# Attention and gated FFN on one core: the value products of units 2 to 11 summed by row tile, the two sums added on VectorE

## The chip, the cores and the metric

The kernel runs on one core of one Trainium2 chip. The metric is the time of one execution on the device in microseconds; a measurement is the median of several runs. The profile shows one execution of its own. Its span runs from the first to the last instruction of the program, and the time of the same execution is a little longer, because of what lies around the program.

The names of the engines are those of the profile: PE (TensorE, matrix products) and PEld (its weight loads), DVE (VectorE), ACT (ScalarE), POOL (GpSimd) and SP (SyncE); the last two issue DMAs here, POOL the loads and SP the transposes and the stores.

## The reference

Block-sparse attention over 4 batches, 8 heads, 768 positions and 64 columns a head, and then a gated feed-forward network (FFN) on the 3072 tokens of 512 columns:

```python
scores = scale * np.matmul(q, k.transpose(0, 1, 3, 2))
# mask: a block's neighbours, the first and last block, three sampled blocks a row
scores = np.where(mask, scores, -1000000000.0)
attn = np.exp(scores - np.max(scores, axis=-1, keepdims=True))
attn = attn / (np.sum(attn, axis=-1, keepdims=True) + 1e-09)
attn_out = np.matmul(attn, v)
...
gate = 1.0 / (1.0 + np.exp(-(x @ w_gate)))     # x: 3072 x 512, w_gate and w_val: 512 x 1536
out = gate * (x @ w_val) @ w_out               # w_out: 1536 x 512
```

## The kernel before

**Units and pairs.** The work is cut into 12 units of 256 query rows (4 batches of 3 units), and each unit into 4 pairs of heads. A pair has three score steps. A step (`Step`) multiplies keys by queries into a PSUM unit of two banks (`qk`, L553), takes the exponential on ACT into a tile `P` (`exp`, L576) and multiplies `P` by the 0/1 mask on DVE (`mul`, L581; unit 0 has its mask added in the scores instead). When the three steps of a pair are done, the value product (`Pair.pv`, L602) multiplies `P` by the values, which carry a column of ones, so that column 64 of each product is the sum of the row. The product has 65 columns for each of 2 heads and 2 row halves. `norm` (L620) takes the reciprocal of the sums on DVE and multiplies them in, reading PSUM and writing the fp16 tile `x16`. For units 2 to 11 a DMA transpose on SP's queue (`Pair.xbar`, L673) then turns `x16` into the FFN's input `xT`; for units 0 and 1 PE transposes it.

**FFN.** `Ffn.f` (L742) makes the gate and the value product of a group of columns, ACT takes a tanh, DVE combines the two (`gate`). `Ffn.y` (L826) multiplies by the last weights, and ACT or DVE copies the result out of PSUM. Units 4 to 11 go through the FFN two at a time.

**Row tiles.** Nearly all matmuls use 64 of the 128 rows of the array, so that two run side by side, one on each half: a row tile. The two tiles running together must write different PSUM banks, and every sum needs both row tiles. So a product is done in two halves (`turns`, L345): in the first half row tile 0 writes bank 0 and row tile 1 writes bank 1, in the second they change banks and add to what is there. Ahead of the second half an empty instruction waits until the first half has left the array (L349). For the value product, each half is 24 matmuls (`value`, L641: two PE tasks of 24, and other tasks may stand between them). In units 0 and 1 the product uses whole columns of 128 rows instead (`whole`, L362).

**PSUM.** There are four units of two banks (`units_ps`, L308). A PE task that begins a product takes one, written in the order as `:slot`; the task marked `free` gives it back. For the value product that is `norm`.

**The order.** Nothing is scheduled at run time. `ORDER` (L40) is a list of the 1173 tasks in the order in which each engine issues its own: a number, a letter where a task may run on one of two engines (`A` for ACT, `D` for DVE), the PSUM slot after a colon, and after `@` the task that a DMA load is held for. `j3`, `j3s` and the like are matmuls on a dummy tile ahead of the real work. Each engine works through its list in turn, and a task waits until what it needs is done. The list was made ahead of time by a planner; the costs written into `plan.add` (for instance 0.66 for a mask product) are what the planner counts with and do nothing at run time.

Of the kernel before, what the change touches and what calls it, by code (L numbers as in the profile page):

```python
# [13 lines left out]
f32 = mybir.dt.float32  # L14
# [8 lines left out]
NT = S // 128  # L23
# [14 lines left out]
FFN_LAG = 3  # L38
VW = 96
ORDER = """  # L40
j3 j3 j3 j3 j3 j3 j3 5A 8D j3 j3s j3s 0 j3s j3s 9:0 j3s j3s 11A 10D j3s 1:1 j3s j3s j3s 12:2 2 3:0
13A 6:1 j3s 32:2 4D 7A 15:1 34:3 33 16D 17:0 18D 97:1 35 30:2 98D 78:0 31 79D 40:3 20:1 22:0 41
36:2 23D 21D 117:0 92@36 37 44:3 118D 25:1 45 54:0 26D 76:2 77D 46:1 55 80:3 27:2 81D 47 50:0 28D
74:3 19 64:1 51 75D 48:2 65 24 66:3 49 60:0 56:1 67D 61 52:2 29 58:3 14 57 53D 89:0 59 86:2 68:1
87 38:3 69D 90 93:1 39 62:2 108:3 94 42:0 63A 109 43D 95:2 70:1 96D 102:0 71D 111:2 103 110 140:3
126:1 105@140 88 112 104 141 84:0 122:2 113 127 85A 142 130:3 128 132:0 123 129 131 72:1 119:2
99:3 73D 237@102 133 120 124 147:1 91 134 100 135 154:2 101 148 157:0 171:3 158 149 155 164:1 172
143:0 156 176:2 144 159 173 165 145 150:0 231:3 177 190:1 170@231 232 178 189@154 121 146@86 161:2
191 125@143 174:3 151A 192 217@108 162 115:0 114@99 175 244:1 186:2 116 204:3 187 205 138 245 139
211:0 82:2 206 212 83D 214:1 233 183:2 136:0 215 218 137D 246 193:0 184 219 194D 152 200:1 216 153  # L50
179:0 220 201 160@200 180D 229 167:2 255:0 166 168 202 272:1 221A 185 256 223A 188 234:2 230 239
307:3 257 181 195 235 273 262 258 197:2 240 213 308 274 198 275 248:0 182 309 199 241:1 249 242
310 196 268:2 169 225:3 250 252:1 224 269 251 226 222 253 227 263 106:0 207:2 107A 254 318:3 208
319 315:0 289:1 209 247@315 316 236 265:3 293:2 260 266 320 261 300:0 290 243 301 238 267 276:3
291 282:0 210 294 283 292 279 277 295 303:1 335:0 278 304 296 297 285:3 336 286 305 228 362:1 163
337 287 363 331:2 264 328:3 348 302 332 270 344:1 329 349 333 345 359:2 284 322:3 203@359 350 364
360 288@197 323 351D 353A 311:1 271@265 426:2 324 312 321@331 427 341:0 373:3 313 342 330 325
397:2 408:1 346 374 398 343 387:0 409 317 370:2 259 375 405:1 388 400@54 406 376 386@40 371 389
355:3 365@157 419:1 390 432@108 356 407 443:0 411@197 420 372 444 347@405 361 433:2 421 334@30 298
357 366:0 306@164 399 377 380:3 434 422 381 299 410 367 435 428 412:1 368 436 454:3 369 413 455  # L60
382 450:2 414 326 471:0 451 472 415 447:3 338 452 401:1 473 440:0 478:2 391 402 441 448 403 479
470 378 457:0 449 280 458 445 394:1 383:2 438 460 395 392 439 456 461 384 396 327 429:0 524:1 385
462 430 459 423 416:2 525 442 484:0 354 465D 463A 481:1 281 417 431 482 485 418 474:3 488:1 486
# [4 lines left out]
583 547 537:3 563:2 314 570 538 586 638:0 552 564 571 539 572 639 565 566:3 577:2 575A 573D  # L68
556@566 595:0 567 576 604 446@32 466 609:1 568 712@86 616:3 596 358 691@64 617 608@46 610 597
641@164 630:3 598 611 622@64 592:0 612 658@282 578 404 593 706:1 579 631 707 594 635:2 561 627:0  # L70
632 543@635 588:1 636 633 628 623:3 629 654 670:2 589 671 618 688:0 624 590 689 591 642:2 453 625
619:1 640 659:0 620 637 643 626 605:1 708 663:3 644 569@605 621 606 660 587@183 645 726@40 681:1
661 709:2 664 676@265 710 662 682 548 665 673:0 549 692:2 683 674 711 699:1 599 666 655:0 693 607
# [3 lines left out]
750 739 751:3 748 752 837:1 650 742 669 749 838 757:3 745D 760 764:0 743D 823:1 758 824 782 667  # L77
759 765 825 826:2 798:1 839 767 827 614 580 734:0 615 799 768 828 753 735 761:2 651 806:1 769 797
762 800 790:0 807 756 862:2 791 736 770A 779 772A 771 819:1 719 763 792 809:3 863 793 810 820 705
# [5 lines left out]
909:0 912 905 910 928 922 913 937 911 855:2 978:0 896 914 856 888 946:1 917A 915D 919:2 947 979  # L85
857 920 929:3 921 938 1027:0 932 875:2 1028 930 948 918 1012:1 876 1013 931 877 970:0 893 1024:2
952:1 939 1025 966 940 971 959:2 953 941 960 942A 1055:0 973:1 961 1056 944D 1001:2 1057 967:0 974
# [6 lines left out]
1074 1081 1093 1089 1082 1065 1094 1083 1084 1095 1085D 1108:1 1096D 1104:0 1098D 1097 1087D 1099  # L94
# [3 lines left out]
1153 1163:0 1156A 1159 1154A 1157 1164 1155 1165 1160 1166 1167 1168:1 1161 1169 1170 1162 1171  # L98
1172
"""  # L100
GAP, PV_HALF, F_HALF, Y_ONE = 0.3, 0.36, 0.875, 0.216
WIDE, WIDE_PV = 1, 2


# [53 lines left out]
def kernel(  # L158
# [231 lines left out]
    def before(nm, i):  # L390

        j = i - len(rings[nm])
        return used[nm][j] if j >= 0 else []
# [196 lines left out]
    class Pair:  # L590
# [50 lines left out]
        def value(self):  # L641
            deps = self.products + [vdone[self.b, self.p]]
            if self.n < WIDE_PV:
                a = plan.add(
                    [(PE, 2 * PV_HALF)],
                    lambda eng: self.pv(None),
                    deps,
                    take=self.bank,
                    ops=48,
                    wide=True,  # L650
                )
# [474 lines left out]
```

## Time and profile before

| | |
|---|---|
| median of 3 runs (lowest, highest) | 281.54 us (281.45, 283.77) |
| the profiled execution, its time | 281.49 us |
| the profiled execution, its span | 279.7 us |
| PE busy | 271.4 us, 97% of the span, 5007 matmuls |
| DVE busy | 188.7 us, 67%, 387 instructions |
| ACT busy | 188.7 us, 67%, 237 instructions |
| granted TensorE clock | 1.00 all through |
| value products of units 2 to 11 | 1920 matmuls of 64 rows by 65 columns |
| last value product starts | at 238.8 us |

How to read it: the 1.8 us between the time and the span lie around the program. Busy PE time is not PE at its peak, because matmuls overlap and their ends are modelled; what a stretch of matmuls costs is read from the distance between starts. A busy share of 67% for DVE and ACT is an average over a start in which data is still arriving, a long middle part in which attention and FFN are mixed, and an end that is FFN alone, where both are nearly idle.

### The profile page before, as it was taken

What the parts mean: (1) busy time and instruction counts of PE and PEld (TensorE: products, weight loads), DVE (VectorE), ACT (ScalarE), POOL (GpSimd) and SP (SyncE); (2) the same over time, 40 slices, a digit from 0 to 9 for tenths busy, and PEclk for the clock granted to TensorE, in tenths of its full rate; (3) what the DMA queues carried; (4) which work ended last, traced back from release to release, by engine and by line L of the source; (5) the groups of instructions that cost most, each with busy time, mean ns of one, the idle gap of its engine ahead of it and who ended that gap; (6) DMA issues with size and microseconds to landing.
All of it is one profiled execution on the core that took longest, in us unless ns stands there. A gap on an engine that the chain in (4) does not pass through costs nothing.

```text
span 279.7 us, 11113 instructions
## 1 busy us (share of the span) xinstructions
PE 271.4 (97%) x5007; PEld 207.6 (74%) x5007; DVE 188.7 (67%) x387; ACT 188.7 (67%) x237; POOL 47.4 (17%) x70
## 2 busy tenths in 40 slices
PE   8799999989999999999999999999999999999995
PEld 4577786977898799658899889888766567555543
DVE  4578777877877988867796897567735787243311
ACT  4899868879957988976877793877779651013411
POOL 7876443010480000071400000000000000000000
PEclk9999999999999999999999999999999999999999
DMA  7999999994699864169596443210110011430003
GB/s 150 180 195 197 200 205 197 149 186 87 83 138 163 102 147 101 40 128 189 72 175 90 58 106 96 68 58 2 41 38 2 0 22 23 143 150 4 0 2 150
DMA packets 56680, 28.93 MB, mean 103 GB/s; under 512 B 33044, under 2 KB 53676, under 8 KB 56632
## 3 DMA queue, kind: packets, MB, share of 16 engines
q0 software_dynamic: 21552, 13.93, 35.9%
q1 hardware_dynamic: 34628, 14.02, 25.7%
q8 instruction: 39, 0.64, 0.9%
q10 hardware_dynamic: 452, 0.26, 0.3%
q14 instruction: 9, 0.07, 0.1%
HBM read 28.47 MB, written 6.29 MB: 124 GB/s over the span
## 4 chain that ended last, share of the span: by engine, by line
PE 92%; DMA 2%; POOL 2%; ACT 1%; DVE 1%; issue 1%; DVEq 0%
PE m L343 91%; DMA k<-in_k_dram 2%; ACT P L577 1%; PE m L463 1%; POOL k L225 1%; POOL q L225 1%; POOL v L225 0%; DVE ysb L856 0%; DVE mask L287 0%; POOL e L262 0%; ACT ysb L854 0%; PE m L458 0%; DVE x L623 0%; DVE e L208 0%; ACT ysb L897 0%
## 5 line engine op out<-in xcount | busy, mean ns | idle before, releaser
L577 ACT ACTIVATE P<-m 128x1024 f16<-128x1024 f32 x144 | 142.2, 1025 | 31.8 <-PE m L343 28.5
L343 PE MATMUL m<-xT,wv 64*128 64x512 f16 (+2 forms) x720 | 136.7, 327 | 0.0
L343 PE MATMUL m<-xT,wg 64*128 64x512 f16 (+2 forms) x720 | 135.4, 327 | 0.0
L583 DVE TENSOR_TENSOR P<-P,mask 128x1024 f16<-128x1024 f16 x132 | 86.0, 686 | 4.4 <-ACT P L577 3.9
L343 PEld LDWEIGHTS <-wg 64*128 64x128 f16 (+1 forms) x720 | 66.6, 94 | 14.1 <-issue 1.5
L343 PEld LDWEIGHTS <-wv 64*128 64x128 f16 (+1 forms) x720 | 66.5, 94 | 11.4 <-issue 0.3
L772 DVE SCALAR_TENSOR_TENSOR ht<-th,m 128x512 f16<-128x512 f32 x72 | 49.2, 686 | 37.4 <-ACT th L769 36.5
L343 PE MATMUL m<-wo,ht 64*128 64x512 f16 (+2 forms) x564 | 71.7, 372 | 0.0
L769 ACT ACTIVATE th<-m 128x512 f32<-128x512 f32 x72 | 42.9, 598 | 40.7 <-PE m L343 37.5
L343 PE MATMUL m<-qT,kT 64*128 64x256 f16 x576 | 56.5, 269 | 0.3 <-issue 0.2
L343 PEld LDWEIGHTS <-P 64*128 64x128 f16 (+1 forms) x2112 | 46.9, 94 | 5.8 <-issue 1.3
L343 PE MATMUL m<-vex,P 64*128 64x65 f16 (+1 forms) x2112 | 48.1, 190 | 0.9 <-issue 0.9
L343 PEld LDWEIGHTS <-ht 64*128 64x128 f16 (+1 forms) x564 | 35.5, 94 | 17.9 <-issue 1.3
L343 PEld LDWEIGHTS <-kT 64*128 64x128 f16 x576 | 33.6, 94 | 9.3 <-issue 1.1
L622 DVE RECIPROCAL rz<-m 128x4 f32<-128x4 f32 x48 | 8.6, 179 | 19.4 <-PE m L343 18.9
L623 DVE TENSOR_TENSOR x<-m,rz 128x256 f16<-128x256 f32 x48 | 20.4, 425 | 1.7
L225 POOL DMA_DIRECT2D q<-in_q_dram x19 | 13.8, 724 | 39.7 <-PE m L343 37.4
L225 POOL DMA_DIRECT2D v<-in_v_dram x16 | 11.6, 734 | 36.1 <-PE m L343 29.7
L225 POOL DMA_DIRECT2D k<-in_k_dram x15 | 10.8, 724 | 9.3 <-PE m L343 4.7
L856 DVE TENSOR_SCALAR ysb<-m 128x512 f32<-128x512 f32 x11 | 7.3, 687 | 7.4 <-PE m L343 5.8
L854 ACT ACTIVATE ysb<-m 128x512 f32<-128x512 f32 x11 | 6.3, 607 | 7.0 <-PE m L343 5.9
L899 DVE TENSOR_SCALAR ysb<-m 128x256 f32<-128x256 f32 (+1 forms) x2 | 1.1, 558 | 7.7 <-PE m L343 7.7
(46 smaller groups left out, 75.9 us busy)
## 6 DMA issues: line engine op xcount, KB each, us to landing
out_dram<-ysb SPq DMA_DIRECT2D x23, 256.0 KB, 2.4
v<-in_v_dram POOLq DMA_DIRECT2D x16, 192.0 KB, 6.4
k<-in_k_dram POOLq DMA_DIRECT2D x15, 192.0 KB, 6.9
q<-in_q_dram POOLq DMA_DIRECT2D x12, 192.0 KB, 7.8
wg<-in_moe_w_gate_dram POOLq DMA_DIRECT2D x6, 256.0 KB, 8.9
wv<-in_moe_w_val_dram POOLq DMA_DIRECT2D x6, 256.0 KB, 10.0
wo<-in_moe_w_out_dram POOLq DMA_DIRECT2D x3, 512.0 KB, 12.7
xT<-x SPq DMA_TRANSPOSE x40, 3.4
```

Source lines behind the costliest of these rows:

```text
L225: return nc.gpsimd.dma_start(dst[:, h0:h1, t0:t1, :], src[b, h0:h1].rearrange("h (p t) d -> p h t d", t=NT)[:, :, t0:t1, :],)
L343: return nc.tensor.matmul(out, lhsT, rhs, start=start, stop=stop, skip_group_check=True).ins
L463: nc.tensor.transpose(out16[a * D : (a + 1) * D, h, i * D : (i + 1) * D], tile_[rows, a], ident[rows, rows],)
L577: nc.scalar.activation(self.pt.rearrange("a h i n -> a (h i n)"), both(self.bank).rearrange("a h n -> a (h n)"), AF.Exp, bias=0.0, scale=SCALE
L583: nc.vector.tensor_tensor(self.pt, self.pt, m.unsqueeze(1).broadcast_to([128, 2, 2, UQ]), op=ALU.mult,)
L622: nc.vector.reciprocal(rz, self.acc[:, :, :, D : D + 1])
L623: nc.vector.tensor_tensor(self.x16.rearrange("a s h d -> a h s d"), self.acc[:, :, :, 0:D], rz.broadcast_to([128, 2, 2, D]), op=ALU.mult,)
L769: nc.scalar.activation(th, both(bank)[:, 0, :], AF.Tanh, bias=0.0, scale=0.5)
L772: nc.vector.scalar_tensor_tensor(self.ht[:, tiles[0] : tiles[-1] + 1, :], in0=th.rearrange("a (f n) -> a f n", n=self.w), scalar=1.0, in1= ...
L854: nc.scalar.activation(ysb, both(bank)[:, s, :], AF.Copy, bias=0.0, scale=0.5)
L856: nc.vector.tensor_scalar(ysb, in0=both(bank)[:, s, :], scalar1=0.5, scalar2=None, op0=ALU.mult)
L899: nc.vector.tensor_scalar(ysb, in0=src, scalar1=0.5, scalar2=None, op0=ALU.mult)
```

## The change

For units 2 to 11 the value product becomes one PE task of 48 matmuls (`pv_parts`). Row tile 0 writes bank 0 throughout and row tile 1 writes bank 1, so that nothing changes banks and the wait between halves is gone. Each bank then holds a part of every sum: 260 columns (2 heads, 2 row halves, 65 columns). A new DVE task (`fold`) adds the two banks column by column, one reduction that reads 520 fp32 columns of PSUM and writes 260 to a tile `acc` in SBUF, and gives the PSUM unit back. `norm` then reads `acc` in SBUF in place of PSUM. Units 0 and 1 stay as they were.

The whole `ORDER` is another one. It holds the same matmuls; five of the FFN's copies out of PSUM that were on DVE are on ACT (16 and 6, where it was 11 and 11), and the copy of the mask rows at the start is on ACT too.

```diff
-        def pv(self, first):
+        def pv(self, eng):
             acc = both(self.bank)[:, :, 0 : 2 * (D + 1)]
...
-            if first is None:
-                whole(mms, self.bank)
-            else:
-                turns(mms, self.bank, first)
+            whole(mms, self.bank)
+
+        def pv_parts(self, eng):
+
+            self.parts = both(self.bank)[:, :, 0 : 4 * (D + 1)]
+            out = self.parts.rearrange("a r (h s d) -> a r h s d", h=2, s=2)
+            for a in range(2):
+                for s in range(2):
+                    for t in range(NT):
+                        for row in range(2):
+                            rows = slice(row * D, (row + 1) * D)
+                            last = tiled(
+                                out[:, row, a, s, :],
+                                self.steps[t // 2].pt[rows, a, t % 2, s * 128 : (s + 1) * 128],
+                                vex[self.b % 2][rows, 2 * self.p + a, t, 0 : D + 1],
+                                (a, s, t) == (0, 0, 0),
+                                (a, s, t) == (1, 1, NT - 1),
+                            )
+            return last
+
+        def fold(self, eng):
+            self.acc = work.tile([128, 2, 2, D + 1], f32, tag="acc", bufs=3, name="acc")
+            nc.vector.tensor_reduce(
+                self.acc.rearrange("a h s d -> a (h s d)"),
+                self.parts.rearrange("a r n -> a n r"),
+                axis=mybir.AxisListType.X,
+                op=ALU.add,
+            )
...
             else:
-                a = plan.add(
-                    [(PE, PV_HALF)],
-                    lambda eng: self.pv(True),
-                    deps,
-                    take=self.bank,
-                    lag=GAP,
-                    ops=48,
-                )
-                a = plan.add([(PE, PV_HALF)], lambda eng: self.pv(False), [a], ops=48)
+                a = plan.add([(PE, PV_PARTS)], self.pv_parts, deps, take=self.bank, ops=96)
...
+            free = self.bank
+            if self.n >= WIDE_PV:
+                a, free = plan.add([(DVE, 0.66)], self.fold, [a], free=self.bank), None
             self.normed = plan.add(
-                [(DVE, 0.6)], self.norm, [a] + before("x16", self.i), free=self.bank
+                [(DVE, 0.6 if free else 0.5)], self.norm, [a] + before("x16", self.i), free=free
             )
```

More of the change, by code (lines that the diff above doesn't have):

```diff
@@ L46 @@
[L46 to L51, printed above, removed]
@@ new lines @@
+38:1 59 90 68:0 39 93:2 69A 52:1 42:3 94 108:0 53A 109 62:1 43D 70:2 63D 102:3 95:1 71D 189@32 103
+111:0 96D 140:2 110 126:1 112 104 141 113 122:3 84:0 127 85A 130:2 128 132:0 123 129 131 119:1
+72:3 99:2 120 133 73D 124 147:3 134 91 100 135 154:1 148 157:2 171:0 155 149 142 158 156 143:3
+164:1 121 176:2 144 92@164 159 172 170@99 88 165 101 161:3 177 173 190:1 162 178 145 150:0 186:3
+191 115:2 151A 192 174:0 187 116 231:1 175 244:2 204:3 232 166 183:0 245 188 205 146@183 233 184
+82:1 217@30 193:2 206 83D 237@64 214:0 194D 234:1 179:2 215 218 114@50 180D 181 136:2 235 246 219
@@ new lines @@
+216 211:0 220 137D 212 152 185 200:1 153 255:2 201 229 138 272:0 213 223A 139 256 221A 195 239 202
+167:1 307:3 168 260 230 273 257 169 240 197:1 308 258 274 198 275 248:2 182 309 199 241:0 249 196
+242 310 268:1 262 225:3 250 163 261 269 251 252:0 226 318:2 263 207:1 319 253 315:3 208 289:0 316
+247@315 236 106:2 160@30 265:1 290 107A 243 266 254 300:3 293:2 209 279 301 227 276:1 270 291 228
+282:3 294 277 283 292 238 335:1 295 278 303:3 296 362:0 297 336 304 284 285:2 363 320 337 267 286
+359:3 331:0 302 348 332 210 328:2 264 349 360 305 350 287 329 361 344:0 322:3 345 203@344 333
@@ new lines @@
+311:2 288@154 323 353A 341:0 321@119 312 387:3 351A 342 346 411@328 426:1 373:2 313 427 317 397:0
+374 343 398 259 408:1 388 375 330 400@60 409 376 370:0 306@231 428 389 419:2 386@303 371 271@60
+355:1 390 405:0 420 356 406 324 380:3 366:1 421 399 432@380 381 407 443:0 334@197 367 422 444
+365@32 433:3 357 368 410 377 454:2 471:0 369 434 455 325 382 412:1 435 364 472 450:2 436 224 413
+392 338 456 440:3 401:0 451 414 441 415 447:2 372 383:1 394:3 402 391 448 384 339 378 429:0 395
+340 449 452 442 430 481:1 524:3 352 385 460 222 482 473 379 478:0 461 326 525 431 457:1 327 462
@@ new lines @@
+445 458 298 484:3 403 479 299 459 467:1 465A 396 485 463A 468 474:0 416:2 486 280 658@474 469 281
+475 515:1 487 347@102 417 527:0 423 488:3 528 476 512:2 516 489 513 483 491:0 517 526 509:3 498:2
[3 rows of a table added]
+537:3 570 551 404 439 424 638:2 538 571 552 425 639 563:1 539 572 583 564 577:3 604 573A 595:2 578
+574 566:1 586 466 609:3 567 555 596 575A 568 616:1 627:0 358 617 565 622@200 610 628 597 569@265
+635:1 598 630:0 611 608@429 636 612 587@200 592:2 691@56 706:3 588:1 593 707 676@474 618 688:2 631
+446@56 689 654 556@426 619:3 579 589 632 712@44 620 633 642:2 543@328 637 590 670:0 641@86 605:3
@@ new lines @@
+643 591 606 708 623:1 671 607 659:3 640 644 709:0 645 624 710 594 681:2 621 625 673:0 660 682 674
+626 663:2 629 661 692:0 675 649 453 655:1 664 662 726@303 599 672 699:3 665 561 656 693 666 646:2
[3 rows of a table added]
+576 749 741 762 760 734:2 742 763 735 703 732 757:3 745A 756 826:2 750 743D 758 827 684 759 779
+838 766 823:0 809:2 767 600 810 668 768 704 669 797 751:1 739 787:2 752 769 788 790:1 772A 770D
[6 rows of a table added]
+910 857 771 919:2 836 927 911 936:0 914 925 937 851 920 929:1 915A 921 978:0 875:2 905 979 917D
+922 930 876 970:0 946:3 932 877 971 1024:2 931 947 1025 893 928 1012:0 1027:3 939 1013 938 959:2
@@ new lines @@
+1028 1040:0 940 1029 1041 960 941 1042 952:3 967:0 944A 973:2 942D 953 943 1001:1 916 968 954 945
[6 rows of a table added]
+1089 1074 1093 1065 1094 1095 1082 1098A 1096A 1083 1097 1120:1 1108:2 1104:0 1109 1121 1110 1105
+1111 1122 1100:2 1123 1084 1101 1087D 1132:1 1085D 1102 1086 1106 1112:3 1103 1099 1107 1088
+1116:2 1133 1117 1134 1113 1135 1118 1128:0 1114 1124:1 1115 1119 1129 1125 1136:3 1126 1130
+1144:2 1131 1137 1127 1140:0 1138 1145 1139 1141 1146 1148:1 1147 1142 1149 1143 1150 1158:3
+1163:2 1164 1165 1151 1166 1167 1152 1153 1159 1156A 1154A 1157 1160 1155 1168:0 1161 1169 1170
@@ L100 @@
+1162 1171 1172
 """
-GAP, PV_HALF, F_HALF, Y_ONE = 0.3, 0.36, 0.875, 0.216
+GAP, PV_HALF, PV_PARTS, F_HALF, Y_ONE = 0.3, 0.36, 0.74, 0.875, 0.216
 WIDE, WIDE_PV = 1, 2
@@ L645, in value @@
                     [(PE, 2 * PV_HALF)],
-                    lambda eng: self.pv(None),
+                    self.pv,
                     deps,
```

36 lines of the change are left out of this document (4 added, 32 removed), and 39 rows, old and new, of the table ORDER.

## The prediction

> **What bounds the kernel now.** I read the page first: busy times and the chain that ended last.
>
> ```profile
> PE 271.4 (97%) x5007; PEld 207.6 (74%) x5007; DVE 188.7 (67%) x387; ACT 188.7 (67%) x237; POOL 47.4 (17%) x70
> ...
> PE 92%; DMA 2%; POOL 2%; ACT 1%; DVE 1%; issue 1%; DVEq 0%
> ```
>
> PE is the bound nearly from end to end, so the change gains only what PE now loses between matmuls. The split into stretches of 20 us shows where that is (the columns are the stretch, its length, and busy us of PE, PEld, DVE, ACT, POOL, then the granted clock).
>
> ```profile
> 40.00:60.00 20.00, 19.29 (x432) 15.98 (x430) 15.36 (x37) 15.04 (x19) 2.81 (x4) 1.00 1.32 184
> 60.00:80.00 20.00, 19.72 (x465) 16.74 (x462) 16.00 (x32) 18.33 (x22) 5.32 (x8) 1.00 0.72 100
> 80.00:100.00 20.00, 19.83 (x477) 16.90 (x475) 16.99 (x38) 15.24 (x19) 3.85 (x6) 1.00 0.96 127
> 100.00:120.00 20.00, 20.00 (x463) 17.06 (x457) 16.80 (x34) 17.75 (x21) 0.00 (x0) 1.00 0.45 94
> ```
>
> The clock is full. From 100 us on PE has no idle time; between 40 and 100 us it has 1.2 us. Then the timeline of PE, to see what a value product costs and what the idle time is.
>
> ```profile
> 145.28 0.38 PE L343 MATMUL m<-xT,wg 64*128 64x512 f16 x1
> 145.40 0.90 PE L343 MATMUL m<-vex,P 64*128 64x65 f16 x45
> 146.13 0.38 PE L343 MATMUL m<-xT,wg 64*128 64x512 f16 x1
> ...
> 56.04 1.17 PE L343 MATMUL m<-vex,P 64*128 64x65 f16 x66
> 57.92 0.63 PE L343 MATMUL m<-vex,P 64*128 64x65 f16 x30 [0.71 <-issue]
> ```
>
> Two halves in a row (48 matmuls, three of them merged apart) take 145.40 to 146.13, 0.73 us: 15.2 ns a matmul, with no cost between. The longest idle time, 0.71 us, lies inside a value product and its releaser is "issue": no engine let PE wait.
>
> I went through the starts of PE's matmuls after 24 us: where a start is over 0.11 us late, the lateness adds up to 2.4 us. Of this 1.8 us lies at four places, instructions 1987, 2242, 3523 and 5313 of PE's stream (0.88, 0.40, 0.35, 0.16 us), multiples of 256 apart within a few. The instruction queue of the trace moved 39 packets of 16 KB, 256 instructions of PE each; ahead of these four places a packet had started only 2.2 to 2.4 us before PE went on. **So PE's largest loss is waiting for its own instructions**, where a block of 256 is used up fast: a value product uses one instruction per 7.6 ns, an FFN product one per 54 ns.
>
> **The change part by part.**
>
> *PE's work.* The built programs have the same 5007 matmuls with the same shapes, so 0. The run of 48 takes 48 x 15.2 = 0.73 us, as the two halves did.
>
> *The waits removed.* A half right behind its first half costs 0.13 us: FFN products start 0.21 apart, and 0.34 apart at 121.21 to 121.55, where the halves touch. But of the 40 pairs the order leaves under 0.3 us of other PE work between the halves in four only, a score product of 0.22 us each, which covers most of it; one such second half starts 0.12 us late (99.11 us): **-0.2 us** (0 to -0.4). The other 36 waits are hidden by FFN or score matmuls already.
>
> *The fold.* 520 fp32 columns of PSUM. The nearest rows are DVE's reads of fp32 PSUM:
>
> ```profile
> L772 DVE SCALAR_TENSOR_TENSOR ht<-th,m 128x512 f16<-128x512 f32 x72 | 49.2, 686 | 37.4 <-ACT th L769 36.5
> L623 DVE TENSOR_TENSOR x<-m,rz 128x256 f16<-128x256 f32 x48 | 20.4, 425 | 1.7
> L622 DVE RECIPROCAL rz<-m 128x4 f32<-128x4 f32 x48 | 8.6, 179 | 19.4 <-PE m L343 18.9
> ...
> L856 DVE TENSOR_SCALAR ysb<-m 128x512 f32<-128x512 f32 x11 | 7.3, 687 | 7.4 <-PE m L343 5.8 <-ACT ysb L854 1.5
> L300 DVE TENSOR_REDUCE mb<-const 24x48 f16<-24x192 f32 x1 | 0.3, 341 | 0.0
> ```
>
> From 425 ns at 256 columns to 687 at 512 is 1.02 ns a column, so 520 columns give 0.695 us. No row reads the two banks in turn, column by column. Lower end 0.43 us (260 columns, both banks at once); upper end 1.2 us (each column at twice the price). I take 0.695: the kernel's one TENSOR_REDUCE, in SBUF, has 1.1 ns a column over L294's (192 columns 341 ns, 72 columns 207 ns).
>
> A rule speaks against this. The Trainium skill, page "Vector Engine (DVE) Microarchitecture Reference", section "Measured stream behaviour on trn2", has a read that hops in SBUF at every element at 1.73 ns a column where neighbours take 1.054, though it excepts a single stream alternating between two regions. By the hop price the fold would be an estimated 1.06 us; no row here shows either.
>
> *norm from SBUF.* 4 columns: 179 to about 150 ns; 256 columns: 425 to about 400 (207 ns at 72 columns plus 184 x 1.04). So -0.05 us a pair (0 to -0.15). The five copies that go to ACT free 5 x 0.60 us.
>
> *Is DVE still cover?* Operations in a row on DVE start 0.08 us before the last one's end (mask products, 686 ns, start 0.60 apart), so a pair adds 0.61 - 0.05 = 0.56 us, 40 pairs 22.4, less 3.0 for the copies and about 1 at the start: DVE busy 188.7 to about 207 us, 74%. By the orders and start-to-start times, DVE's work beside 60 us of PE work in the middle (PE's matmuls 40 to 100 us into its work) rises from 49.2 to 55.3 us, 92%. It still fits. The chain to the FFN (0.29 us until the product is read, fold, norm 0.6, transpose 3.4 by the DMA rows: 5.0 us) has at least 6.3 us of PE work beside it in the new order. The tightest place is the PSUM unit: the fold must end before the next product takes it. That needs 0.29 + 0.695 + 0.06 = 1.05 us; the new order leaves 0.95 once, 1.08 ten times, 1.17 to 1.3 seven times, more in 22. Norm needed 0.96 us against 0.84 once, 1.08 five times. So the fold hardly ever stops PE, but there is less slack when a mask product (0.60 us) is in front of it: **+0.5 us** (0 to +3).
>
> *The order: instructions.* How soon a block is used up is read from the PE work in the 300 instructions ahead of its end, each matmul at its start-to-start time. In the new order the four bad places have 5.5 and 4.3 us (unchanged), 5.9 (was 6.5) and 6.5 (was 6.7). There the fetch started 3.4 to 4.8 us after PE was at the first of the 300, and PE went on 2.2 us after that at the earliest, 5.6 to 7 us in all. So all four come back and the third is longer; three other blocks get tighter (4803rd instruction 6.0 to 4.9, 7107th 6.7 to 4.0, 8131st 6.8 to 5.1), where fetches started after only 1 to 2 us. **+0.5 us** (0 to +2).
> The skill's page "Runtime: NRT & Kernel Launch", section "Instruction fetch mechanics", calls the cost of crossing such a block mostly hidden. The trace's 0.71 us speaks against it here; by the page this term would be 0.
>
> *The order: start.* Matmuls of 64 and of 128 rows change places 38 times in place of 36, at 0.10 us (starts 0.21 apart at 25.43 to 25.64, 0.11 within): **+0.2 us**. The copy of the mask rows now stands ahead of the first exponential on ACT, so that starts about 0.8 us later (6.90 to 7.7), but ACT waited 1.08, 0.30 and 0.50 us later on in the start, for scores behind the third and fourth k loads, and the new order has scores ready there. I take **0** (-1 to +1).
>
> *POOL and SP* issue the same loads and transposes; the loads of later batches wait for PE tasks as before, long ahead of use.
>
> **Sum**: -0.2 + 0.5 + 0.5 + 0.2 + 0 = +1.0 on the profiled execution's 281.49 us (279.7 span and 1.8 around it), which is 0.05 under the median: **282.5 us**. One per cent, 2.8 us, is about what a measurement here can tell from no change.
>
> **The rivals.**
> *DVE becomes the bound because the fold reads slowly.* At 1.2 us it needs 1.55 us where 18 folds leave 0.95 to 1.3: each lets PE wait about 0.4 us, 7 us; and 16 folds add 8 us to the 55.3 in the middle 60, 3 us too much, part of the same wait. Some 288 us. It decides from a fold of about 0.8 us on, where the 11 tightest places open. For it: the alternating banks; against: every fp32 PSUM row has the same slope. By the skill's hop rule (above) the fold alone would need an estimated 1.06 us, a milder form of this.
> *PE stops for instructions more often.* Runs of 48 packed before block ends, or loads that share the DMA engines at the wrong moment: another two blocks at 0.9 us and the start 1 us worse, about 285.5 us. For it: 0.88 us in one place now; against: the equal density.
> *A gain.* The fetches fall well (-1.8), the halves' waits go (-0.4), the start gains 1 us: 278.3 us. For it: each is a loss that the trace shows; against: nothing in the new order spreads the value products.
>
> **How the numbers follow.** Forecast, within 1%: 0.70. Slow fold 0.14, more instruction stops 0.09 (both slower by over 1%). Gain 0.07. So faster 0.07, same 0.70, slower 0.23. The range: the lower ends of the terms (-0.4 + 0 + 0 + 0.2 - 1) give 280.3, and I go to 279.7 for part of the gain; the upper ends together (+3, +2, +0.2, +1) would be 287.7, seldom all at once; 286.5 leaves out the worst of the slow fold.
>
> **What would show it.** The fold's row near 695 ns, x40; value products in runs of 48 with 0.73 us to the next start; DVE busy 203 to 211 us; PE idle by "issue" inside value products near 57, 62 and 89 us again; first exponential near 7.7 us, first FFN product within 1 us of the 24.2 of now. I am wrong if the fold takes over 0.8 us, if PE shows idle time by DVE in the middle, or if the start moves by over 1 us.

## The result

The changed kernel takes 280.82 us (median of 21 runs) where the kernel before takes 281.99 us beside it. The ratio is **0.995, with an interval of 0.9933 to 0.9968**: a gain of 1.2 us, by the interval 0.3 to 0.7%. The forecast was 282.5 us, a loss of 1.0 us on the profiled execution. The time lies inside the forecast's range and within its one per cent, but on the other side of no change, and what was to cost 1.0 us gained 1.2. The question of this part is which term was wrong.

The page of the changed kernel: busy times, the chain that ended last, and the rows of the fold (L637) and of `norm` (L646, L647).

```profile
PE 271.2 (97%) x5007; PEld 183.3 (66%) x5007; DVE 208.2 (75%) x421; ACT 192.1 (69%) x243; POOL 47.3 (17%) x70
...
PE 86%; DMA 5%; ACT 4%; DVE 1%; POOL 1%; issue 1%; SPq 0%; DVEq 0%; ACTq 0%
...
L637 DVE TENSOR_REDUCE acc<-m 128x260 f32<-128x520 f32 x40 | 27.8, 697 | 7.1 <-PE m L343 6.4
...
L647 DVE TENSOR_TENSOR x<-acc,rz 128x256 f16<-128x256 f32 x40 | 17.0, 425 | 1.4
...
L646 DVE RECIPROCAL rz<-acc 128x4 f32<-128x4 f32 x40 | 6.9, 172 | 0.2
```

The fold takes 697 ns, as worked out (695). DVE's busy time is 208.2 us (207 was forecast). `norm` gained almost nothing from reading SBUF: 425 and 172 ns, where it had 425 and 179. In the chain ACT and DMA have taken shares from PE: there are waits now that were not there before.

The split into stretches of 20 us, same columns as before.

```profile
40.00:60.00 20.00, 20.00 (x456) 15.92 (x454) 16.66 (x36) 17.11 (x22) 3.48 (x5) 1.00 1.13 175
60.00:80.00 20.00, 20.00 (x495) 16.22 (x491) 18.72 (x40) 17.48 (x23) 6.38 (x10) 1.00 0.63 88
80.00:100.00 20.00, 19.53 (x467) 15.48 (x463) 18.66 (x40) 16.51 (x22) 3.53 (x5) 1.00 0.99 155
100.00:120.00 20.00, 19.87 (x481) 15.89 (x475) 17.96 (x38) 17.28 (x21) 0.00 (x0) 1.00 0.56 91
```

Between 40 and 80 us PE, which had lost 1.0 us, has no idle time left. Between 80 and 120 us it has 0.6 us, where it had 0.2. DVE works 55.3 of the 60 us from 60 to 120 us: the 92% of the prediction. The timeline of PE shows the places themselves, first the value products near 57 us, then the longest wait.

```profile
56.25 1.62 PE L343 MATMUL m<-vex,P 64*128 64x65 f16 x96
57.71 0.38 PE L343 MATMUL m<-qT,kT 64*128 64x256 f16 x4
...
97.84 0.84 PE L343 MATMUL m<-vex,P 64*128 64x65 f16 x44 [0.47 <-ACT ysb L873]
```

Two runs of 48 take 56.25 to 57.71, 0.73 us each, and nothing stops in or behind them. The stop for instructions that stood near 57 us is gone, and with it those at 62, 89 and 128 us. In their place are waits for ACT and DVE, the largest at 97.84 us.

**The bookkeeping.** As in the prediction I take every start of a PE matmul that is over 0.11 us late, from the first FFN product on. A *stop at a block end* is one at the end of a block of 256 PE instructions (the 193rd to 195th after a multiple of 256) with the fetch of the next block begun 2.2 to 2.9 us before PE goes on. The rest are waits for other engines and DMAs. All later kernels are counted the same way (us).

| kernel | median, ratio to the kernel before | span of the profiled execution | stops at block ends | other late starts | first FFN product |
|---|---|---|---|---|---|
| before | 281.99 | 279.7 | 1.78 | 0.6 | 24.2 |
| before, second profile | 282.2, 0.998 | 281.5 | 3.39 | 0.7 | 24.5 |
| after | 280.82, 0.995 | 279.3 | 0.30 | 1.9 | 24.5 |
| after, second profile | 281.0, 0.996 | 279.6 | 0.76 | 1.7 | 24.5 |

So between the two first profiles and between the two second ones the stops fell by 1.5 and 2.6 us, the other waits grew by 1.3 and 1.0, and the start lost 0.3 and 0.0; delays under 0.11 us each, which sum to 2.0 to 2.2 us before, sum to 1.7 to 1.8 after. The spans differ by 0.4 and 1.9 us, and the 1.2 us of the medians lie between. Nothing ties a profile of one kernel to one of the other: in the crossed pairs the stops fell by 1.0 and 3.1 us.

### The profile page after: what moved, and what is told of

Read it like the earlier page. It is cut to its first block, busy times and chain, and to the rows that moved or that the text cites. A ratio compares the mean times of both kernels' runs of the same rounds, so it can differ in the third digit from the quotient of the medians.

```text
span 279.3 us, 11165 instructions
## 1 busy us (share of the span) xinstructions
PE 271.2 (97%) x5007; PEld 183.3 (66%) x5007; DVE 208.2 (75%) x421; ACT 192.1 (69%) x243; POOL 47.3 (17%) x70
## 4 chain that ended last, share of the span: by engine, by line
PE 86%; DMA 5%; ACT 4%; DVE 1%; POOL 1%; issue 1%; SPq 0%; DVEq 0%; ACTq 0%
PE m L343 86%; ACT P L577 3%; DMA k<-in_k_dram 2%; DMA out_dram<-ysb 1%; DMA kT<-kp 1%; ACT ysb L873 1%; DVE ysb L875 1%; PE m L463 0%; DVE P L583 0%; POOL k L225 0%; POOL q L225 0%; POOL e L262 0%; POOL v L225 0%; ACT qT L285 0%; DVE x L647 0%
## 5 line engine op out<-in xcount | busy, mean ns | idle before, releaser
L343 PE MATMUL m<-wo,ht 64*128 64x512 f16 (+2 forms) x564 | 70.3, 372 | 0.0
L343 PE MATMUL m<-qT,kT 64*128 64x256 f16 x576 | 52.7, 269 | 0.7 <-ACT P L577 0.3
L343 PEld LDWEIGHTS <-ht 64*128 64x128 f16 (+1 forms) x564 | 30.1, 94 | 22.7 <-issue 1.1
L343 PEld LDWEIGHTS <-P 64*128 64x128 f16 (+1 forms) x2112 | 41.3, 94 | 5.1 <-issue 1.1
L343 PE MATMUL m<-vex,P 64*128 64x65 f16 (+1 forms) x2112 | 42.6, 190 | 0.5 <-ACT ysb L873 0.5
L343 PEld LDWEIGHTS <-kT 64*128 64x128 f16 x576 | 27.8, 94 | 15.7 <-issue 1.6
L637 DVE TENSOR_REDUCE acc<-m 128x260 f32<-128x520 f32 x40 | 27.8, 697 | 7.1 <-PE m L343 6.4
L225 POOL DMA_DIRECT2D v<-in_v_dram x16 | 11.5, 727 | 58.5 <-DVE vex L536 34.3
L873 ACT ACTIVATE ysb<-m 128x512 f32<-128x512 f32 x16 | 9.2, 600 | 17.7 <-PE m L343 16.8
L647 DVE TENSOR_TENSOR x<-acc,rz 128x256 f16<-128x256 f32 x40 | 17.0, 425 | 1.4
L225 POOL DMA_DIRECT2D q<-in_q_dram x19 | 13.6, 717 | 24.9 <-PE m L343 23.8
L225 POOL DMA_DIRECT2D k<-in_k_dram x15 | 10.8, 722 | 3.0 <-PE m L343 2.5
L646 DVE RECIPROCAL rz<-acc 128x4 f32<-128x4 f32 x40 | 6.9, 172 | 0.2
```

Of the source, the lines that this page charges most:

```text
L225: return nc.gpsimd.dma_start(dst[:, h0:h1, t0:t1, :], src[b, h0:h1].rearrange("h (p t) d -> p h t d", t=NT)[:, :, t0:t1, :],)
L343: return nc.tensor.matmul(out, lhsT, rhs, start=start, stop=stop, skip_group_check=True).ins
L637: nc.vector.tensor_reduce(self.acc.rearrange("a h s d -> a (h s d)"), self.parts.rearrange("a r n -> a n r"), axis=mybir.AxisListType.X, o ...
L646: nc.vector.reciprocal(rz, self.acc[:, :, :, D : D + 1])
L647: nc.vector.tensor_tensor(self.x16.rearrange("a s h d -> a h s d"), self.acc[:, :, :, 0:D], rz.broadcast_to([128, 2, 2, D]), op=ALU.mult,)
L873: nc.scalar.activation(ysb, both(bank)[:, s, :], AF.Copy, bias=0.0, scale=0.5)
```

## The experiments

Two theories. **Placement:** the gain is in which work and which DMA traffic happen to stand ahead of the ends of the instruction blocks; the value product's new form only came with another order. **The run of 48:** the gain comes from the new form, with its waits gone.

### One part of the change alone

The changed kernel with the order of the kernel before; the fold takes the place of the second half:

```diff
 ORDER = """
-j3 j3 j3 j3 j3 j3 j3 j3 8A 5D j3s 0 6:0 j3s j3s 7A j3s 9:1 j3s 11A j3s 10D j3s 1:2 j3s 12:0 2 3:1
+j3 j3 j3 j3 j3 j3 j3 5A 8D j3 j3s j3s 0 j3s j3s 9:0 j3s j3s 11A 10D j3s 1:1 j3s j3s j3s 12:2 2 3:0
...
```

> The new value product, fold and norm, in the old order: the run of 48 matmuls stands where the first half stood, the fold where the second half stood, norm where it was. If the gain of 0.5% comes from the run itself (no change of banks, PSUM given back after the fold), it is here too: 0.993 to 0.997 of the kernel before. If it comes from the new order alone, this is 0.999 to 1.010 of before, slower where folds in the old places let PE wait, because the old order has no room for 24 us more of VectorE work.

Measured: 287.04 us, ratio 1.0201 (1.0161 to 1.0241), slower than either expectation. PE starts late by 7.7 us in all, at many places; the largest are 0.63 us at 74.59 us, behind a copy on ACT, 0.73 at 204.06, behind a fold, and 0.86 at 240.87, behind a mask product on DVE. In an order that was not made for the fold, the new form costs 5 us.

The other way round: two halves, no fold, the new order, with the second half where the fold stood and `norm` right behind it (three transposes stand earlier so that each task follows what it needs). One pair in the order, whose tasks are 252 (value product or first half), 253 (fold or second half) and 254 (norm):

```diff
-252:0 226 318:2 263 207:1 319 253 315:3 208 289:0 316 247@315 236 106:2 160@30 265:1 290 107A 243 266 254
+252:0 226 227 318:2 263 207:1 319 253 254 315:3 208 209 289:0 316 247@315 236 106:2 160@30 265:1 290 107A 243 266
```

> The old halves in the new order: the second half stands where the fold stood and norm right behind it; three transposes of x are moved up so that norm finds its tile free. If the gain comes from the new order (instruction blocks arrive in time at the 1987th, 2242nd and 3523rd instruction), this is 0.993 to 0.998 of before. If it comes from the run of 48, this is 1.000 to 1.010: many second halves now stand right behind their first and pay 0.13 us each.

Measured: 299.65 us, ratio 1.0659 (1.0611 to 1.0706), far above either expectation. What PE waited for:

```profile
PE m L343 <- DVE x L623: 12.4, 20, 2.0
```

The order takes the PSUM unit again right behind the fold's place, and here only `norm` gives it back. That is a cost of where the second half stands, so the halves were then put together: the second right behind the first, and `norm`, reading PSUM, where the fold was.

```diff
-252:0 226 318:2 263 207:1 319 253 315:3 208 289:0 316 247@315 236 106:2 160@30 265:1 290 107A 243 266 254
+252:0 253 227 318:2 263 207:1 208 319 254 315:3 209 289:0 316 247@315 236 106:2 160@30 265:1 290 107A 243 266
```

> The new order with the value product in two halves and no fold: the second half stands right behind the first, norm stands where the fold stood and reads PSUM. My reading: each of the 40 second halves waits about 0.13 us for the first half to leave the array, 5.2 us in all, while norm (0.6 us) does for the PSUM unit what the fold (0.7 us) did and DVE has 28 us less to do, which gives back about 0.5 to 1 us: 285 to 287 us, ratio 1.012 to 1.018. If two halves close together cost nothing, 280 us.

Measured: 290.16 us, ratio 1.0292 (1.0261 to 1.0322), more than either expectation. The timeline of PE:

```profile
56.99 2.10 PE L343 MATMUL m<-vex,P 64*128 64x65 f16 x96
58.94 0.38 PE L343 MATMUL m<-qT,kT 64*128 64x256 f16 x4
```

The same two products take 1.95 us instead of 1.46. Nearly every second half starts 0.225 us late (not 0.13); 40 of them are 9.0 us. So in an order that leaves nothing between the halves **the run of 48 is worth 9 us**. It gained next to nothing against the kernel before, because that one's order already hid nearly all of these waits, as the prediction had read. The run of 48 allows the new order; the 1.2 us are not waits between halves.

### The blocks shifted

Small dummy matmuls ahead of the real work move every later PE instruction on, and with it the work that stands at a block end. First 32 of them in a wait for the third keys:

```diff
-20:1
+j1p16 20:1
...
+        if kind[:1] == "p":
+            for x in range(int(kind[1:])):
+                for i in range(2):
+                    rows = slice(i * D, (i + 1) * D)
+                    nc.tensor.matmul(
+                        units_ps[unit][:, i, 0:64], junk[rows], junk[rows, 0:64], start=True, stop=True
+                    )
+            return
```

> The kernel before with 32 dummy matmuls of 64 columns (64 instructions with their weight loads) while PE waits for the third pair's k, at 9.4 to 10.6 us. They take about 0.5 us of a wait of 1.1 us. Theory of the instruction blocks: everything behind lies 64 instructions later in its block, the stops move to other work, and the 1.8 us lost at the four places changes: 0.994 to 1.004 of before, with PE's stops again at the instruction numbers 195 over a multiple of 256 (1987, 2243, ...). Rival, that the stops at these places come from something in the work there (a late load, a late product): the same stops at the same work, 64 instruction numbers on, and 0.999 to 1.002.

> The changed kernel with the same 32 dummy matmuls in the wait for the third pair's k. Theory of the instruction blocks: the place in the blocks is what made the changed kernel win, so that with another place its gain changes by 0.5 to 2 us: 0.991 to 1.003 of before. If the gain has nothing to do with the blocks: 0.994 to 0.997, as without the dummies.

Measured: 282.6 us, 1.0039 (1.0013 to 1.0065), for the kernel before and 282.44 us, 1.0027 (0.9998 to 1.0056), for the changed one. The stops moved: 1.64 us in one place before, 2.77 us in four places after, none at the old work. The dummies also delayed the start, by 2.0 us in the first and 0.4 us in the second, which blurs the comparison of the two. So the next two shifts replace some of the first dummies instead, where PE waits for the first data anyway: two of them by 16 pairs (56 instructions more), or four by 32 pairs (112 more).

```diff
-j3 j3 j3 j3 j3 j3 j3
+j3p16 j3 j3 j3 j3 j3
```

> The kernel before, with 32 small dummy matmuls in place of 2 of the first dummies ahead of the real work: every later PE instruction stands 56 places further on. Alignment theory (PE's losses are set by which work happens to lie ahead of the end of a block of 256 PE instructions): the start is the same within 0.3 us, the four stops of the kernel before (1.78 us together) leave their work; by the PE work in the 300 instructions ahead of each block end, the end near instruction 2243 now has 4.0 us (was 5.6) and is the worst, a stop of 1 to 2 us there, 1 to 3 us of stops in all; time within 1 us of the kernel before. Rival (the new order and the runs of 48 are what is faster, alignment does not matter): the stops stay at their work or sum up to the same, and the shifted changed kernel is 1 to 1.3 us faster than this one.

> The changed kernel, shifted by 56 PE instructions in the same way. Alignment theory: the block end near 2243 has 3.0 us of PE work in its 300 instructions (was 4.1) and stops PE for 1 to 2 us, in all 1 to 3 us of stops where the changed kernel has 0.3; the time is 0.7 to 2 us above the changed kernel, that is 281.5 to 283, and within 0.7 us of the shifted kernel before. Rival: under 0.5 us of stops, 280.8 us, still 1 us or more below the shifted kernel before.

> The kernel before shifted by 112 PE instructions (64 small dummies for 4 of the first). Alignment theory: block ends with little PE work ahead of them are 2243 (3.9 us), 4291 (4.4), 3267 (4.4), 8131 (4.3); 1 to 3 us of stops at some of these; time within 1 us of the kernel before. Rival: as for the shift of 56, 281.8 us, 1 us or more above the changed kernel with the same shift.

> The changed kernel shifted by 112 PE instructions. Alignment theory: block ends with little work ahead are 2243 (2.9 us), 3267 (4.5), 4291 (4.9), 2499 (5.0); 1 to 3 us of stops, 281.5 to 283 us, and the mean of the shifted changed kernels (64, 56, 112) is within 0.6 us of the mean of the shifted kernels before. Rival: 280.8 us, 1 us or more below the kernel before with the same shift.

| kernel | median, ratio to the kernel before | span | stops at block ends | other late starts | first FFN product |
|---|---|---|---|---|---|
| before + 56 | 281.41, 1.0001 (0.9975 to 1.0027) | 279.4 | 1.93 | 0.5 | 24.1 |
| after + 56 | 281.55, 0.9983 (0.9954 to 1.0013) | 279.6 | 0.86 | 1.8 | 24.3 |
| before + 64 | 282.6, 1.0039 | 281.4 | 1.64 | 0.6 | 26.3 |
| after + 64 | 282.44, 1.0027 | 281.4 | 2.77 | 1.0 | 24.9 |
| before + 112 | 283.58, 1.0063 (1.0039 to 1.0088) | 281.9 | 3.73 | 0.8 | 24.6 |
| after + 112 | 282.65, 1.0031 (1.0008 to 1.0055) | 280.9 | 2.81 | 1.4 | 24.1 |

Every stop again stood 193 to 195 instructions behind a multiple of 256, whatever the work was; the place expected to be the worst, 2243, was so in each of the four (0.59 to 1.56 us). A shift that changes no work moves either kernel by up to 2 us, which is more than the change did. With 112 the changed kernel gives back its whole gain, and the kernel before takes 1.5 us more, where at most 1 us was expected. Side by side, the changed kernel is ahead by 0.2, 0.1 and 0.3% at 56, 64 and 112 by the ratios, with intervals that overlap at each, in place of 0.5% without a shift; the means of the three medians are 282.5 and 282.2 us. At 64 the start flatters it: the kernel before begins its first FFN product 1.4 us later there, and with that taken off, an estimate, the changed one would be 1.2 us behind. So most of the gain goes with a shift that changes no work. That all of it does is not shown.

### The two kernels again

> The kernel before, unchanged, for a second profiled execution and as the yardstick of this group. If the stops for instructions depend on where the block ends lie and on the order of the DMAs, which are the same, they stand at the same four instructions (1987, 2242, 3523, 5313) with 1.8 us together (within 0.6); ratio 1.000 within 0.003. If they depend on chance from one execution to the next, other places or a sum that differs by over 1 us.

> The changed kernel, unchanged, for a second profiled execution. By place: under 0.6 us of stops for instructions again, at 4291 and little else, waits for DVE at the same works (97.8, 122.9, 164.5, 207.7 us), and a ratio to before of 0.995 (0.993 to 0.998). By chance: stops of 1 to 2 us at other places, ratio anywhere from 0.993 to 1.002.

Measured: 282.2 us and 281.0 us; the changed kernel's ratio is 0.9961 (0.994 to 0.9981). The kernel before itself has 0.998 (0.9954 to 1.0007) in this group, so that a difference of 0.2% can come from the group alone. It had its stops at exactly the same four instructions, but with 1.07, 0.68, 0.90 and 0.74 us, 3.39 in place of 1.78. What PE waited for in this execution:

```profile
PE m L343 <- issue: 2.6, 4, 0.9
```

The two profiled executions of the kernel before took 281.49 and 283.28 us; of the 1.79 us between them 1.61 are these stops. So **the place is fixed, and the size is not**: in both executions PE went on 2.2 to 2.6 us after the fetch had started, so the size follows the start of the fetch. That also explains why the first pair of profiles differs by only 0.4 us in span: they caught the kernel before with small stops.

### The loads ahead of the fetch

What delays a fetch? PE at the 300th instruction before a block end is about when a fetch can begin: where the DMA engines have little to do, it mostly starts 0.6 to 1.3 us later (up to 2.8 us late in the kernel, where PE uses few instructions and nothing hangs on it). At the four bad places of the kernel before it started 4.1, 3.4, 4.8 and 4.3 us later. In the changed kernel the same four blocks' fetches started 1.0, 1.2, 3.7 and 1.4 us later, in its second execution 2.1, 1.0, 3.0 and 1.2. The third came just in time: PE had 6.1 us of work from that point and went on 2.4 us after the fetch had started. For the fourth the timeline of POOL, which issues the loads, shows why. Before, then after:

```profile
120.67 0.70 POOL L225 DMA_DIRECT2D q<-in_q_dram  x1 [36.82 <-PE m L343]
121.36 0.71 POOL L225 DMA_DIRECT2D v<-in_v_dram  x1
```

```profile
123.31 1.41 POOL L225 DMA_DIRECT2D v<-in_v_dram  x2 [24.23 <-DVE vex L536]
```

PE reaches the 300th instruction at 121.55 us before and at 119.51 us after. Before, eight loads are issued around that moment; after, the first of them comes 3.8 us behind it, and the fetch has begun by then, at 120.85 us. To test it, loads were moved and nothing else, so that PE's instructions keep their numbers. In the order a load's `@` names the score product that releases it; 347 and 306 were issued at 81.7 and 83.1 us, and now follow 512, the others follow 706.

```diff
-347@405
...
-306@164
...
+347@512 306@164
...
-712@86 691@64 608@46 641@164 622@64 658@282
...
+712@706 691@64 608@46 641@164 622@64 658@282
```

> The kernel before, same PE instructions in the same places; two input loads that are issued at 81.7 and 83.1 us go behind the scores near 101 us, and six that are issued from 122.1 to 125.5 us go behind the scores near 126 us. If the loads on the DMA engines are what makes the fetches late: the fetch for the block end at 3523 starts near 85.5 us in place of 87.3 to 88.3, the one at 5315 near 123 in place of 125.9 to 127.6, the stops of PE there (0.35 and 0.16 us in one execution, 0.90 and 0.74 in the other) vanish, those at 1987 and 2242 stay; 0.5 to 1.6 us below the kernel before, ratio 0.994 to 0.998. If not: the stops stay, ratio 1.000.

Measured: 283.17 us, ratio 1.004 (1.0015 to 1.0064): slower, against the expectation. The timeline of PE and of POOL:

```profile
111.04 0.39 PE L343 MATMUL m<-vex,P 64*128 64x65 f16 x14
113.10 0.33 PE L343 MATMUL m<-vex,P 64*128 64x65 f16 x10 [1.67 <-issue]
```

```profile
103.80 1.40 POOL L225 DMA_DIRECT2D v<-in_v_dram  x2 [20.99 <-PE m L343]
```

The stop at 5315 went. But the two loads held back came 1.7 us before PE stood 300 instructions ahead of the end near 4547, a place that had never stopped in this kernel: the fetch there began 5.2 us later instead of 1.2, and PE stopped for 1.84 us (one profiled execution). At 3523 the stop grew to 1.43 us. The loads left in front of it still filled the DMA engines until 87.0 us, and transposes that had queued behind them then went ahead of the fetch. So my estimate of how soon the engines would be clear was wrong, while the cause is confirmed by the stop that two loads made.

The same in the changed kernel, whose one stop, at 4291, had two loads in front of it, issued at 97.7 and 98.4 us:

```diff
-658@474
...
-347@102
...
+658@553 347@102
```

> The changed kernel with the two loads of 97.7 and 98.4 us behind the scores near 104.6 us. If loads make the fetch late: the fetch for the block end at 4291 starts near 99.5 us in place of 101.9 to 102.7, the stop there (0.30 and 0.76 us in two executions) goes, 0.3 to 0.8 us below the changed kernel: 280.1 to 280.6, ratio to before 0.992 to 0.995. If not: the stop stays.

Measured: 280.99 us, ratio 0.9966 (0.9944 to 0.9988). The fetch for 4291 began 0.92 us after the 300th instruction (3.6 and 4.1 us in the two executions of the changed kernel), the next one 0.98 (3.0 and 3.6), and no stop at a block end is left. PE at 4291, in the second execution of the changed kernel and then here:

```profile
105.00 0.28 PE L343 MATMUL m<-xT,wg 64*128 64x256 f16 x1 [0.59 <-issue]
```

```profile
104.42 0.27 PE L343 MATMUL m<-xT,wg 64*128 64x256 f16 x1
```

The mechanism is as expected; the time is not better. That the stop is missing would not show it alone. In the run with the shorter fold below, the two loads stand where they stood in the changed kernel, the fetch came 2.3 us after the 300th instruction, and PE did not stop there either. In the run with the fold done twice they are issued just as PE reaches that instruction, as in the second execution of the changed kernel, and the fetch came 1.0 us after it, not 4.1. So loads near a fetch do not always hold it up; what else is on the DMA engines at that moment may decide, and no run varied that alone. In this execution the start was 0.6 us later, and the other waits are 1.3 us. Then one more load, released earlier:

```diff
-203@344
+203@328
```

> As the run before, and the value load of 71.0 us released by an earlier score product, 1.9 us sooner. The copy of these values on DVE waited 0.3 and 1.1 us for the load in two executions, and PE after it 0.13 and 0.87 us (77.2 us, a wait for DVE and no fetch). Expected: this wait under 0.2 us, another 0.1 to 0.7 us gained: 279.6 to 280.4. If the earlier loads delay another fetch instead (the block end at 3011 has 1.6 us to spare), no gain.

Measured: 280.53 us, ratio 0.9956 (0.9927 to 0.9986), span 278.8. The wait at 77 us went (0.13 and 0.87 us before), and another one grew:

```profile
97.81 0.88 PE L343 MATMUL m<-vex,P 64*128 64x65 f16 x47 [0.94 <-ACT ysb L873]
```

Its lateness was 0.62 us in the first execution of the changed kernel, none in the second, which had lost 0.87 us at 77 us; here it is 1.1 us, and at 3523 there is a stop of 0.2 us. PE comes to 97 us earlier and waits there for a copy by ACT that is no earlier. Part of what a stop costs is thus free: it is spent out of a wait that follows. This version is not shown to be faster than the changed kernel.

### The fold made shorter and longer

```diff
-                self.parts.rearrange("a r n -> a n r"),
+                self.parts[:, 0:1].rearrange("a r n -> a n r"),
```

> The changed kernel, the fold reading one bank's 260 columns only (the other row tile's part of every sum is left out of the result): PE's instructions and the order as they are, the fold about 0.43 us in place of 0.70. If the fold's length is what makes PE wait in the middle (about 1.8 us by DVE and ACT in the changed kernel, of it some 1.1 us where DVE was the last to finish), those waits shrink by 0.7 to 1.2 us and the time is 0.7 to 1.2 us below the changed kernel: 279.6 to 280.1. If DVE has room anyway and the fold costs nothing, within 0.4 us of the changed kernel.

Measured: 280.36 us, ratio 0.9932 (0.9909 to 0.9955), 0.5 to 0.6 us below the changed kernel. This kernel leaves out half of every sum; only its time is of use.

```profile
L637 DVE TENSOR_REDUCE acc<-m 128x260 f32<-128x260 f32 x40 | 17.0, 425 | 9.8 <-PE m L343 9.0
```

The waits at 97.8 and 122.9 us of the first execution of the changed kernel, 1.0 us together, are not there. But they are not there in its second execution either, which like this one waits at 78 us instead. PE in that second execution, and then with the shorter fold:

```profile
78.16 0.27 PE L343 MATMUL m<-xT,wg 64*128 64x256 f16 x1 [0.71 <-DVE ht L791]
```

```profile
77.68 0.27 PE L343 MATMUL m<-xT,wg 64*128 64x256 f16 x1 [0.72 <-DVE ht L791]
```

Against that second execution the late starts other than at block ends are the same, 1.7 us, and what is missing here is the stop at 4291 (0.76 us) and 0.3 us at the start. So half of the fold and 10.8 us less of DVE work bring some half a microsecond at best, and the traces do not show that even this comes from the fold's length.

```diff
+            for _ in range(2):
                 nc.vector.tensor_reduce(
...
```

> The changed kernel with every fold done twice in a row: 0.64 us more until the PSUM unit is free, DVE busy about 234 us (84%). By the prediction's slack (1.17 to 1.3 us left at the tightest 18 places, over 1.3 at 22) and by the middle 60 us (DVE's 55.3 us of work there becomes about 65): the tight places each wait 0.4 to 0.6 us and the middle does not fit by 5 us, 287 to 292 us. If the new order has far more room than the prediction counted, below 284.

Measured: 298.02 us, ratio 1.0552 (1.0526 to 1.0579), above the range expected. Its fold row, what PE waited for, and DVE's share from 60 to 120 us:

```profile
L638 DVE TENSOR_REDUCE acc<-m 128x260 f32<-128x520 f32 x80 | 55.3, 696 | 6.8 <-PE m L343 4.9
```

```profile
PE m L343 <- DVE acc L638: 10.4, 24, 1.0
```

```profile
60.00:120.00 60.00, 55.44 (x1310) 46.62 (x1311) 58.52 (x117) 46.09 (x57) 10.49 (x15) 1.00 0.61 101
```

DVE is full (58.5 of 60 us), and PE waits for the PSUM unit of the fold itself 24 times. From 425 to 697 ns the fold costs some 0.5 us at most, from 697 to 1393 ns it costs 17 us. The order has room for the fold that it was made for and hardly more.

## Why the prediction was wrong, point by point

- **The order: instructions (+0.5): this is the step that failed.** "So all four come back and the third is longer": none came back. Measured is -1.5 and -2.6 us in the two pairs of profiles. The working judged a block end by PE's work in the 300 instructions ahead of it and took the lateness of the fetch, 3.4 to 4.8 us in the trace of before, as if it belonged to the place. It follows the DMA traffic, and the new order moved that too. Traffic alone, moved with PE's instructions in place, made a stop of 1.84 us (loads held back in the kernel before) and brought the fetch for 4291 forward from 3.6 and 4.1 us to 0.9 (loads held back in the changed kernel). The three blocks that I said get tighter (4803, 7107, 8131) did not stop PE, as I had argued. The term's lower bound should have been the -1.8 us that the trace showed; I left that to the rival *a gain* at 0.07.
- That rival named "the fetches fall well (-1.8)", and that part is what happened. Its two other parts were not: the halves' waits were hidden, and the start did not gain.
- The Trainium skill's page "Runtime: NRT & Kernel Launch", section "Instruction fetch mechanics", calls the crossing of a block mostly hidden. Most were: some 35 of 39 cost nothing here. But by the page the kernels would not differ in this, and in these runs the crossings cost 0 to 4.6 us.
- **DVE and the PSUM unit (+0.5): not contradicted, and not shown.** The kernel with half the fold's length is 0.5 to 0.6 us faster, but what its profile lacks is a stop at a block end, its late starts behind DVE are those of the second execution of the changed kernel, and in neither profile of the changed kernel does a wait of PE end with the fold. Other late starts grew by 1.0 to 1.3 us in all, by waits for DVE, ACT and loads at new places; for those on ACT and loads the prediction had no term. That the PSUM unit is the tight place shows only with the fold twice as long.
- **The fold (0.695 us): 0.697.** In this row a column that takes both banks in turn has the price of the other fp32 columns of PSUM. The hop price of the Trainium skill's page "Vector Engine (DVE) Microarchitecture Reference", section "Measured stream behaviour on trn2", gave an estimated 1.06 us and does not apply here. The page itself excepts a stream that alternates between two regions, and the measured row agrees with that exception.
- **norm (-0.05 a pair): -0.01.** The estimate took SBUF rows of other sizes; the source made no difference.
- **The waits removed (-0.2): about right**, 0.1 to 0.2 us, as they were hidden before. A wait that is not hidden is 0.225 us, not 0.13.
- **The start (0, -1 to +1): right.** The first exponential starts at 7.63 us (7.7 was forecast), the first FFN product at 24.5 us in both executions, 0.0 to 0.3 later.
- **The mode changes (+0.2): not seen.** The delays under 0.11 us, where they would show, fell by 0.2 to 0.5 us.
- **The slow fold** did not come. Its point of decision lies, as stated, above 0.7 us, and its price was too low: 7 us for a fold 0.5 us longer, where the run with 0.7 us more lost 17.

What stays open: how much of the 1.2 us would survive an order tuned anew for block ends (the shifts leave 0.1 to 0.3%, with intervals that overlap). Whether the new order was made with the block ends in view, or fell well by luck, the record does not say; the plan does give each PE task its number of instructions (`ops=96`). Nor was it tried which transfers made the stop at 1987, the largest in the kernel before. The DMA packets of the traces name a candidate: a load of values issued at 47.49 us still had packets until 54.97 us, among transposes, and the fetch started at 55.51; in the changed kernel the loads there had ended at 50.76 us, and the fetch started at 52.67 among transposes alone. Why the same stop measures 0.35 us in one execution and 0.90 in the next is open too.

## What to carry to other kernels

When a change moves the whole order of a long kernel, its losses by instruction fetch are new ones: they depend on the work just ahead of each block end and on the transfers that stand in front of the fetch, so the term needs a range on both sides of zero, as wide as the loss that the trace shows now. Look at two profiled executions before taking the size of a stop from one. A wait that other work hides in one order can be worth 9 us in another, and an operation that fits at 0.7 us can cost 17 us at 1.4: such a price holds only for the order at hand.

## What was not expected of the hardware

- PE's stops for instructions stood at 193 to 195 behind a multiple of 256 in every run, with any work there, and PE never went on sooner than 2.2 us after the fetch of the next block had started. The fetch mostly started 0.6 to 6 us after PE was 300 instructions ahead, the latest where loads and transposes filled the DMA engines.
- Two 192 KB loads, issued 1.7 us before that point, were enough for a stop of 1.84 us.
- A second half directly behind the first of a value product costs 0.225 us each time.
- PEld's busy time fell from 207.6 to 183.3 us with the same 5007 weight loads at the same 94 ns. These would add up to 471 us one by one, so overlapping loads count once, and this number says nothing of the work.
